# Block 0's second product split at 8 of 16 tiles of d_ff, and the transfers and casts around it put in another order

## The chip, the cores and the metric

The kernel runs on one core of a Trainium2 chip. The core has five engines that run side by side, each through its own instructions in order: TensorE (PE in the profile; PEld is its weight load), VectorE (DVE), ScalarE (ACT), GpSimd (POOL) and SyncE (SP), which here only issues DMA transfers. The metric is the device time of one execution in microseconds, the lower the better.

## The reference

Two parts follow each other. The first is a recurrent retention layer over 4 batches, 8 heads, 768 positions and a head dimension of 64; the second is a two-layer network over the 3072 resulting rows of 512, with d_ff = 2048:

```python
for t in range(S):
    state = gamma * state + k[t] (outer) v[t]        # per batch and head, 64 x 64
    y[t] = q[t] @ state / sqrt(D)
x = y.transpose(0, 2, 1, 3).reshape(3072, 512)
h = x @ w_in                                         # 512 -> 2048
g = maximum(h, 0) + alpha * minimum(h, 0)
out = g @ w_out                                      # 2048 -> 512
```

## The kernel before

All matmuls are in float16. The recurrence is computed in chunks: inside a chunk a masked product of q and k (the scores) is multiplied with v, and a state of 64 x 64 per head is carried from chunk to chunk. The 3072 rows are six blocks of 512 tokens. Blocks 0 and 1 are made of the units 0 to 3, each of 256 positions, two to a block; the later blocks are made of units of 128 positions that are numbered from 8.

For a unit of 256 positions the steps are: `uload` (three transfers of 512 KB for k, q and v), `uscaled` (k and q times powers of gamma, cast to float16 in tile `ukq`, four products on POOL for units 2 and 3), a turn of `ukq` into `ukT` (for unit 2 by transposing matmuls, `uturn`, whose banks are copied out by DVE and ACT; for unit 3 by two transposing transfers, `uturn_dma`), `ucast` (v to float16, ACT), `uscores` (PE, reads `ukT`), `umasked` (DVE, writes `um`), `ustates` and `usums` (the state), and `uoutputs` (PE, then copies into `xT`, which is the input of the network).

For a block of 512 tokens the first product `x @ w_in` runs over 16 tiles of d_ff (`ffn1`, `ffn1_half`; ACT makes `hm`, DVE makes the tile `gt`, `gs` for block 0). The second product of block 0 is cut in two: `ffn2_start` takes the first tiles of d_ff, summed in four banks of PSUM, one for each 128 rows, and ACT copies the four sums to `os`; `ffn2(0, lo=...)` takes the other tiles, and DVE adds the sums to `os`. Between the two parts stands the first half of block 1's first product. For blocks 1 to 5 the second product is `seven`, seven smaller products on sums of quarters of `g` (`g_sums`) and of w_out (`w_sums`: wsum0 from tiles 0 to 7, wsum1 and wsum2 in two halves each, wsum3).

The weights arrive as float32 in quarters of 1 MB, each as two transfers of 512 KB (`load_w`), and are cast to float16 by POOL (`cast_w`, four casts for a quarter). Quarter i of w_out holds the tiles 4i to 4i + 3 of d_ff. All of these loads, the transposing transfers and the stores are issued by SP in one order and go through one queue; the float32 data of loads and weights share a ring of 12 buffers of 512 KB.

The order of the work is written out by hand: each engine executes in the order of the lines of the kernel. The products are generators that yield after every matmul, and `tick(gen, m)` puts m of these matmuls between other work. Thus in `ffn2_start` the number of ticks ahead of `uturn`, `uscores`, `ustates` and `uoutputs` says how many of its matmuls PE does before each of them. An engine that stands at an instruction whose input is not there yet does nothing else meanwhile.

Of the kernel before, what the change touches and what calls it, by code (L numbers as in the profile page):

```python
# [19 lines left out]
def kernel(  # L20
# [310 lines left out]
    def uload(w, nms="kqv", parts=1):  # L331
        b, c = divmod(w, NCH // 2)
        for nm in nms:
            src = {"k": k, "q": q, "v": v}[nm]
            t = ring(f"{nm}u{w}").rearrange("p (h j d) -> p h j d", j=2, d=D)
            for r in range(2):
                ustaged[w, nm, r] = t[:, 4 * r : 4 * r + 4]
            n = H // parts
            for h in range(0, H, n):
                nc.sync.dma_start(  # L340
                    out=t[:, h : h + n],
                    in_=src[b, h : h + n, 256 * c : 256 * c + 256, :].rearrange(
                        "h (p j) d -> p h j d", j=2
                    ),
                )

    def uscaled(w, nm, r, eng):
        if w not in ukq:
            ukq[w] = sbp.tile([128, 2, 2, 4, 2, D], F16, tag="ukq", bufs=2, name=f"ukq{w}")
            ukT[w] = sbp.tile([128, 2, 4, 2, 128], F16, tag="ukT", bufs=2, name=f"ukT{w}")  # L350
            uv[w] = sbp.tile([128, 2, 4, 2, D], F16, tag="uv", bufs=2, name=f"uv{w}")
        a = "kq".index(nm)
        at = 32 + 16 * a + 8 * r
        eng.tensor_tensor(  # L354
            out=ukq[w][:, a, :, :, r, :].rearrange("p j i d -> p i j d"),
            in0=ustaged.pop((w, nm, r)),
            in1=tab[:, at : at + 8]
            .rearrange("p (i j) -> p i j", j=2)
            .unsqueeze(3)
            .to_broadcast([128, 4, 2, D]),  # L360
            op=MULT,
        )
# [34 lines left out]
    def uturn_dma(w):  # L397
        by_dma.add(w)
        for a in range(2):
            nc.sync.dma_start_transpose(  # L400
                out=ukT[w][:, a].rearrange("p i x n -> p (i x n)").rearrange(
                    "p (b n) -> p b n", n=128
                ),
                in_=ukq[w][:, a].rearrange("p j i r d -> p (j i r d)"),
            )
# [187 lines left out]
    def uoutputs(w):  # L593
        z = [None if w % (NCH // 2) == 0 else ps("za"), ps("zb")]
        uout_states(w, 1, z=z)
        zc = [b and z_copy(b).rearrange("p (a j n) -> p a j n", j=2, n=64) for b in z]
        uout_inner(w)
        uout_states(w, 0)
        uout_copy(w, z=zc)
# [128 lines left out]

    def ffn2_start(n):
        banks = [ps("ops", tag="pb") for _ in range(UB)]  # L730
        for f0 in range(0, 12, 4):
            for tq in range(UB):
                for ft in range(f0, f0 + 4):
                    nc.tensor.matmul(  # L734
                        out=banks[tq],
                        lhsT=gt_at(n, ft, slice(128 * tq, 128 * tq + 128)),
                        rhs=w_out_all[:, ft, :],
                        start=(ft == 0),
                        stop=(ft == 11),
                    )  # L740
                    if ft == 11:
                        os_sb = sbp.tile([128, d_model], FP, tag="os", bufs=5, name="os")
                        nc.scalar.activation(
                            out=os_sb, in_=banks[tq], func=COPY, bias=0.0, scale=1.0
                        )
                        partial[n, tq] = os_sb
                    yield
# [12 lines left out]
    def w_sums(which, eng, parts=None):  # L760
        i = which
        if i not in wsum:
            tag, bufs = (("ws0", 1), ("ukq", 2), ("ukT", 2), ("ukT", 2))[i]
            wsum[i] = sbp.tile([128, HF, 256], F16, tag=tag, bufs=bufs, name=f"wsum{i}")
        n = HF if parts is None else HF // 2
        for p in [0] if parts is None else parts:
            w_sum(i, eng, slice(n * p, n * p + n))
# [259 lines left out]
    def tick(gen, m):  # L1027
        for _ in range(m):
            if next(gen, 1) == 1:
                return  # L1030
# [21 lines left out]
    def load_w(nm, i, parts=2):  # L1052
        n = 4 // parts
        for j in (0, 2):
            t = ring(f"{nm}{i}{j}").rearrange("p (j d) -> p j d", j=2)
            if nm == "wi":
                src = wi[:, j : j + 2, 512 * i : 512 * i + 512]
            else:
                src = wo[:, 4 * i + j : 4 * i + j + 2, :]
            for jj in range(0, 2, n):  # L1060
                nc.sync.dma_start(out=t[:, jj : jj + n], in_=src[:, jj : jj + n])
            for jj in range(2):
                wst[nm, i, j + jj] = t[:, jj]

    def cast_w(nm, i, engs):
        left = [j for j in range(4) if (nm, i, j) in wst]
        for j, eng in zip(left, engs):
            to = w_in_all[:, j, 512 * i : 512 * i + 512] if nm == "wi" else w_out_all[:, 4 * i + j, :]
            t = wst.pop((nm, i, j))
            if eng is nc.scalar:  # L1070
                eng.activation(out=to, in_=t, func=COPY, bias=0.0, scale=1.0)
            else:
                eng.tensor_copy(out=to, in_=t)  # L1073
# [17 lines left out]
    V, G, A = nc.vector, nc.gpsimd, nc.scalar  # L1091
# [56 lines left out]
    busy(2, tag="pb")  # L1148
    uturn(1, "k", shared=True, first=A)
    ucast(0, 0, A)  # L1150
    load_w("wo", 1)
    busy(2, tag="pb")
    uturn(1, "q", shared=True)
    umasked(0, 1, sc[1], rs=(1,))
# [30 lines left out]
                pass  # L1185
    cast_w("wi", 2, [G, G, G, G])
    cast_w("wi", 3, [G, G, G, G])
    load_w("wo", 2)
    cast_w("wo", 0, [G, G, G, G])
    cast_w("wo", 1, [G, G, G, G])  # L1190
    uscaled(2, "k", 0, G)
    uscaled(2, "k", 1, G)
    uscaled(2, "q", 0, G)
    uscaled(2, "q", 1, G)
    uload(3)
    load_w("wo", 3)
    for _ in ffn1(0, lo=4):
        pass
    w_sums(0, V)
    gen = ffn2_start(0)  # L1200
    ucast(2, 0, A)
    ucast(2, 1, A)
    cast_w("wo", 2, [G, G, G, G])
    tick(gen, 24)
    uturn(2, "k", tag="pa", shared=True)
    tick(gen, 6)
    uturn(2, "q", tag="pa", shared=True)
# [1 line left out]
    sc = [uscores(2, 0), uscores(2, 1)]  # L1209
    umasked(2, 0, sc[0])  # L1210
    umasked(2, 1, sc[1])
    tick(gen, 4)
    ustates(2, tag="pa")
    usums(2)
    uscaled(3, "k", 0, G)
    uscaled(3, "k", 1, G)
    uscaled(3, "q", 0, G)
    uscaled(3, "q", 1, G)
    uturn_dma(3)
    for u in range(8, 11):  # L1220
        load(u)
    tick(gen, 5)
    uoutputs(2)
    ucast(3, 0, A)
    ucast(3, 1, A)
    w_sums(1, G, [0])
    cast_w("wo", 3, [G, G])
    w_sums(2, G, [0])
    cast_w("wo", 3, [G, G])
    for _ in gen:  # L1230
        pass
    gen = ffn1_half(1, 0)
# [8 lines left out]
    scaled(9, "q", G)  # L1241
    scaled(10, "k", G)
    scaled(10, "q", G)
    sc = [uscores(3, 0), uscores(3, 1)]
    umasked(3, 0, sc[0])
    tick(gen, 8)
    umasked(3, 1, sc[1])
    scaled(8, "k", A)
    cast(8, A)
# [1 line left out]
    turn(9)  # L1251
    load(11)
    turn(10)
    adds = []
    last = ffn2(0, lo=12, late=adds)
    tick(last, 13)
    uoutputs(3)
    flush(adds)
    cast(9, A)
    for _ in last:  # L1260
        pass
# [185 lines left out]
```

## Time and profile before

| | us |
|---|---|
| median of 3 runs (lowest, highest) | 197.95 (197.07, 199.46) |
| the profiled execution's own time | 198.98 |
| its span, first to last instruction | 197.0 |
| PE busy in the span | 189.3 |
| POOL busy | 147.5 |
| DVE busy | 151.3 |
| ACT busy | 121.7 |

The span of the profiled execution is 2.0 us shorter than its time. PE is the engine that is busy for most of the span, so that time is lost only where PE waits; the tensor clock was granted in full throughout. The other engines have idle time, but what they deliver late makes PE wait. Queue q1, on which SP issues, moved 37.36 of the 38.78 MB.

### The profile page before, as it was taken

The page shows a single profiled execution, that of the slowest core. Times are in us where ns is not written, and L with a number is a line of the kernel's source. Part 1 is how long each engine was busy: PE and PEld are TensorE (multiplying, and loading weights), DVE is VectorE, ACT ScalarE, POOL GpSimd, SP SyncE. Part 2 cuts the span into 40 slices and gives each one's busy share as a digit, 9 for nine tenths or more (in the row PEclk, how much of TensorE's full clock was granted, in tenths as well). Part 3 has the DMA queues.
Part 4 walks back from the last instruction along what each step waited for, and adds up shares of the span by engine and source line. Part 5 has one row for each costly group of instructions (what it writes and reads, how often), then busy time and mean ns, then how long its engine had stood idle before and what let it go on. Part 6 is the DMA issues. An engine that isn't in the chain of part 4 may idle for free.

```text
span 197.0 us, 6461 instructions
## 1 busy us (share of the span) xinstructions
PE 189.3 (96%) x2668; PEld 131.7 (67%) x2668; DVE 151.3 (77%) x260; ACT 121.7 (62%) x272; POOL 147.5 (75%) x148
## 2 busy tenths in 40 slices
PE   7789899999999989999999999999999999999993
PEld 5657444557768878744688754788754888654882
DVE  2597889253999698588897879968879977799943
ACT  3368664349687863476458988749987433687120
POOL 3286788999996955999659999579999397589000
PEclk9999999999999999999999999999999999999999
DMA  6999999999999989899999999993890011200014
GB/s 168 310 336 350 404 396 296 332 358 179 210 230 148 214 257 272 196 215 299 196 231 228 226 185 265 237 221 93 113 263 2 3 57 63 100 3 0 2 57 160
DMA packets 92749, 38.78 MB, mean 197 GB/s; under 512 B 70176, under 2 KB 88624, under 8 KB 92720
## 3 DMA queue, kind: packets, MB, share of 16 engines
q1 hardware_dynamic: 91440, 37.36, 77.2%
q10 hardware_dynamic: 1280, 1.01, 1.5%
q8 instruction: 21, 0.34, 0.7%
q14 instruction: 8, 0.07, 0.1%
HBM read 27.35 MB, written 6.29 MB: 171 GB/s over the span
## 4 chain that ended last, share of the span: by engine, by line
PE 73%; SPq 10%; DMA 7%; POOL 6%; DVE 1%; issue 1%; POOLq 0%
PE ops L809 30%; PE hps L942 16%; PE hps L632 12%; PE hps L972 5%; SPq L340 4%; SPq L117 4%; DMA wi<-in_moe_w_in_dram 4%; PE ops L734 4%; POOL wsum L757 3%; DMA kqs<-in_q_dram 3%; PE ya L293 1%; PE yb L293 1%; POOL gs L757 1%; DVE gs L757 1%; POOL ukq L354 1%; PE sca L234 1%
## 5 line engine op out<-in xcount | busy, mean ns | idle before, releaser
L809 PEld LDWEIGHTS <-gt 128*128 128x128 f16 x320 | 30.6, 98 | 4.2
L942 PE MATMUL hps<-xT,win 128*128 128x512 f16 x144 | 33.0, 379 | 0.0
L929 DVE SCALAR_TENSOR_TENSOR gt<-hm,small,hps 128x512 f16<-128x512 f32 (+1 forms) x42 | 28.7, 706 | 5.1 <-ACT hm L925 3.8
L809 PE MATMUL ops<-wout,gt 128*128 128x256 f16 x240 | 28.4, 273 | 0.0
L925 ACT ACTIVATE hm<-hps 128x512 f32<-128x512 f32 x39 | 23.1, 593 | 6.1 <-PE hps L942 5.4
L632 PE MATMUL hps<-xT,win 128*128 128x512 f16 x112 | 24.7, 379 | 0.6 <-POOL win L1073 0.6
L137 POOL TENSOR_TENSOR kq<-kqs,tab 128x512 f16<-128x512 f32 x23 | 23.7, 1051 | 1.9 <-DMA kqs<-in_q_dram 1.9
L642 DVE SCALAR_TENSOR_TENSOR gt<-hm,small,hps 128x512 f16<-128x512 f32 x28 | 20.9, 748 | 3.8 <-ACT hm L641 0.9
L942 PEld LDWEIGHTS <-win 128*128 128x128 f16 x144 | 14.1, 98 | 14.5
L641 ACT ACTIVATE hm<-hps 128x512 f32<-128x512 f32 x28 | 16.7, 597 | 8.9 <-PE hps L632 8.6
L674 DVE SCALAR_TENSOR_TENSOR gt<-hm,small,hps 128x256 f16<-128x256 f32 x40 | 16.9, 476 | 5.0 <-ACT hm L669 5.0
L827 ACT ACTIVATE kept<-ops 128x512 f32<-128x512 f32 x15 | 9.0, 597 | 18.8 <-PE ops L809 18.7
L632 PEld LDWEIGHTS <-win 128*128 128x128 f16 x112 | 10.9, 98 | 13.6 <-POOL win L1073 1.1
L809 PE MATMUL ops<-wsum,gs 128*128 128x256 f16 x160 | 19.0, 273 | 0.7 <-DVE gs L757 0.7
L217 POOL TENSOR_TENSOR t<-ss,tab 128x256 f16<-128x256 f32 x13 | 8.7, 669 | 13.6 <-DVE ss L215 13.6
L757 POOL TENSOR_TENSOR gt<-gt,gs 128x1024 f16<-128x1024 f16 x8 | 17.0, 2126 | 2.2 <-DVE gs L757 2.2
L660 PE MATMUL hps<-xT,win 128*128 128x256 f16 x160 | 18.4, 273 | 0.0
L129 ACT ACTIVATE kq<-kqs,tab 128x64 f16<-128x64 f32 x72 | 18.0, 336 | 0.0
L660 PEld LDWEIGHTS <-win 128*128 128x128 f16 x160 | 15.4, 98 | 2.6 <-DVE xT L584 0.3
L809 PEld LDWEIGHTS <-gs 128*128 128x128 f16 x160 | 15.1, 98 | 3.0 <-DVE gs L757 1.0
L669 ACT ACTIVATE hm<-hps 128x512 f32<-128x512 f32 x20 | 11.8, 597 | 4.5 <-PE hps L660 4.4
L839 DVE TENSOR_TENSOR os<-ops,kept 128x512 f32<-128x512 f32 (+1 forms) x17 | 10.5, 624 | 5.0 <-ACT kept L827 3.7
(139 smaller groups left out, 391.5 us busy)
## 6 DMA issues: line engine op xcount, KB each, us to landing
out_dram<-os SPq DMA_DIRECT2D x20, 256.0 KB, 3.6
wi<-in_moe_w_in_dram SPq DMA_DIRECT2D x8, 512.0 KB, 8.6
wo<-in_moe_w_out_dram SPq DMA_DIRECT2D x8, 512.0 KB, 8.7
kqs<-in_k_dram SPq DMA_DIRECT2D x16, 256.0 KB, 4.4
kqs<-in_q_dram SPq DMA_DIRECT2D x16, 256.0 KB, 4.3
vs<-in_v_dram SPq DMA_DIRECT2D x16, 256.0 KB, 4.7
ku<-in_k_dram SPq DMA_DIRECT2D x4, 256.0 KB, 4.4
qu<-in_q_dram SPq DMA_DIRECT2D x4, 256.0 KB, 5.3
```

Source lines behind the costliest of these rows:

```text
L129: eng.activation(out=kqs[u][:, a, h % 4, h // 4, :], in_=staged[u][nm][:, h, :], func=COPY, bias=0.0, scale=tab[:, H * a + h : H * a + h + 1],
L137: eng.tensor_tensor(out=kqs[u][:, a].rearrange("p i r d -> p r i d"), in0=staged[u][nm].rearrange("p (r i) d -> p r i d", i=4), in1=tab[:, ...
L632: nc.tensor.matmul(out=hps, lhsT=w_in_all[:, hp, 128 * ft : 128 * ft + 128], rhs=xT[n][:, :, hp, :], start=(hp == 0), stop=(hp == 3),)
L641: nc.scalar.activation(out=hm, in_=hps, func=RELU, bias=0.0, scale=-1.0)
L642: nc.vector.scalar_tensor_tensor(out=gt_at(n, ft, slice(0, TB)), in0=hm, scalar=oma_sb[:, ft : ft + 1], in1=hps, op0=MULT, op1=ADD,)
L660: nc.tensor.matmul(out=hps[:, 256 * (ft - f0) : 256 * (ft - f0) + 256], lhsT=w_in_all[:, hp, 128 * ft : 128 * ft + 128], rhs=xT[n][:, half ...
L674: nc.vector.scalar_tensor_tensor(out=gt_at(n, f, to), in0=hm[:, at], scalar=oma_sb[:, f : f + 1], in1=hps[:, at], op0=MULT, op1=ADD,)
L757: eng.tensor_tensor(out=out, in0=a, in1=b, op=op)
L809: nc.tensor.matmul(out=bk[:, 256 * t : 256 * t + 256], lhsT=a[:, f, 128 * t : 128 * t + 128], rhs=w[:, f, :], start=first and f == 0 and ( ...
L925: nc.scalar.activation(out=t, in_=src, func=RELU, bias=0.0, scale=-1.0)
L929: nc.vector.scalar_tensor_tensor(out=gt_at(n, f, cols), in0=hm, scalar=oma_sb[:, f : f + 1], in1=src, op0=MULT, op1=ADD,)
L942: nc.tensor.matmul(out=hps, lhsT=w_in_all[:, hp, 128 * ft : 128 * ft + 128], rhs=x[:, :, hp, :], start=(hp == 0), stop=(hp == 3),)
```

## The change

Block 0's second product is cut after 8 instead of 12 of the 16 tiles: `ffn2_start` has 32 matmuls instead of 48, and `ffn2(0, lo=8)` has 32 instead of 16. The number of matmuls, copies and adds is the same. With `ffn2_start` shorter, unit 2's steps stand after fewer of its matmuls: 3 ahead of `uturn` for k (24 before), then 6, 4, 5 (4 before) and 6 (5 before). Unit 3's scores stand after 54 instead of 48 matmuls of the first half of block 1's first product, and its outputs after 18 of the 32 matmuls of `ffn2(0, lo=8)` (13 of 16 before). The delayed add of `tq == 2` goes.

On the side of the transfers, w_out's second quarter is loaded after unit 2 instead of ahead of it, unit 3 is loaded right behind that quarter, and unit 3's two transposing transfers stand between the third and the fourth quarter instead of behind the fourth. POOL's casts and products follow that order. The sum wsum0, on DVE, moves from ahead of `ffn2_start` to behind unit 2's outputs.

```diff
     def ffn2_start(n):
         banks = [ps("ops", tag="pb") for _ in range(UB)]
-        for f0 in range(0, 12, 4):
+        for f0 in range(0, 8, 4):
...
-                        stop=(ft == 11),
+                        stop=(ft == 7),
                     )
-                    if ft == 11:
+                    if ft == 7:
...
     ucast(0, 0, A)
-    load_w("wo", 1)
     busy(2, tag="pb")
...
     cast_w("wi", 3, [G, G, G, G])
-    load_w("wo", 2)
+    load_w("wo", 1)
+    uload(3)
     cast_w("wo", 0, [G, G, G, G])
-    cast_w("wo", 1, [G, G, G, G])
     uscaled(2, "k", 0, G)
     uscaled(2, "k", 1, G)
     uscaled(2, "q", 0, G)
     uscaled(2, "q", 1, G)
-    uload(3)
-    load_w("wo", 3)
+    cast_w("wo", 1, [G, G, G, G])
+    load_w("wo", 2)
     for _ in ffn1(0, lo=4):
         pass
-    w_sums(0, V)
     gen = ffn2_start(0)
     ucast(2, 0, A)
     ucast(2, 1, A)
-    cast_w("wo", 2, [G, G, G, G])
-    tick(gen, 24)
+    uscaled(3, "k", 0, G)
+    uscaled(3, "k", 1, G)
+    uscaled(3, "q", 0, G)
+    uscaled(3, "q", 1, G)
+    uturn_dma(3)
+    load_w("wo", 3)
+    tick(gen, 3)
     uturn(2, "k", tag="pa", shared=True)
     tick(gen, 6)
     uturn(2, "q", tag="pa", shared=True)
...
     umasked(2, 1, sc[1])
-    tick(gen, 4)
+    tick(gen, 5)
     ustates(2, tag="pa")
     usums(2)
-    uscaled(3, "k", 0, G)
-    uscaled(3, "k", 1, G)
-    uscaled(3, "q", 0, G)
-    uscaled(3, "q", 1, G)
-    uturn_dma(3)
+    cast_w("wo", 2, [G, G, G, G])
     for u in range(8, 11):
         load(u)
-    tick(gen, 5)
+    tick(gen, 6)
     uoutputs(2)
+    w_sums(0, V)
     ucast(3, 0, A)
     ucast(3, 1, A)
     w_sums(1, G, [0])
-    cast_w("wo", 3, [G, G])
     w_sums(2, G, [0])
-    cast_w("wo", 3, [G, G])
+    cast_w("wo", 3, [G, G, G, G])
     for _ in gen:
         pass
...
+    tick(gen, 6)
     sc = [uscores(3, 0), uscores(3, 1)]
     umasked(3, 0, sc[0])
-    tick(gen, 8)
+    tick(gen, 2)
     umasked(3, 1, sc[1])
...
-    adds = []
-    last = ffn2(0, lo=12, late=adds)
-    tick(last, 13)
+    last = ffn2(0, lo=8)
+    tick(last, 18)
     uoutputs(3)
-    flush(adds)
     cast(9, A)
```

The order in which SP issues transfers, from w_out's second quarter to the first loads of unit 8, was this; `wo10` and `wo12` are the two halves of quarter 1 of w_out, `ku2` is k of unit 2, `ukT3` the turned k and q of unit 3, `kqs8` k and q of unit 8:

```order
L1061 DMA wo10_267<-in_moe_w_out_dram 128x2x512
L1061 DMA wo12_269<-in_moe_w_out_dram 128x2x512
L340 DMA ku2_464<-in_k_dram 128x8x128
L340 DMA qu2_466<-in_q_dram 128x8x128
L340 DMA vu2_468<-in_v_dram 128x8x128
L1061 DMA wo20_592<-in_moe_w_out_dram 128x2x512
L1061 DMA wo22_594<-in_moe_w_out_dram 128x2x512
L340 DMA ku3_611<-in_k_dram 128x8x128
...
L1061 DMA wo30_617<-in_moe_w_out_dram 128x2x512
L1061 DMA wo32_619<-in_moe_w_out_dram 128x2x512
L400 DMA_TRANSPOSE ukT3_872<-ukq3_871 128x8x128 x2
L117 DMA kqs8_880<-in_k_dram 128x8x64
```

SP's order at the same place is now this:

```order
L340 DMA qu2_462<-in_q_dram 128x8x128
L340 DMA vu2_464<-in_v_dram 128x8x128
L1061 DMA wo10_588<-in_moe_w_out_dram 128x2x512
L1061 DMA wo12_590<-in_moe_w_out_dram 128x2x512
L340 DMA ku3_592<-in_k_dram 128x8x128
...
L1061 DMA wo20_613<-in_moe_w_out_dram 128x2x512
L1061 DMA wo22_615<-in_moe_w_out_dram 128x2x512
L400 DMA_TRANSPOSE ukT3_716<-ukq3_715 128x8x128 x2
L1061 DMA wo30_724<-in_moe_w_out_dram 128x2x512
L1061 DMA wo32_726<-in_moe_w_out_dram 128x2x512
L117 DMA kqs8_856<-in_k_dram 128x8x64
```

Each of the units 2 and 3 has one quarter of w_out fewer ahead of it, and the two transposing transfers have passed the fourth quarter; whatever stands behind `wo32` has the same transfers ahead of it as before.

On POOL, from unit 3's products (`ukq3`) to the first product of unit 8 (`kq8`), the order was this:

```order
L354 TENSOR_TENSOR ukq3_871<-ku3_611,tab_63 128x4x2x64 x2
L354 TENSOR_TENSOR ukq3_871<-qu3_613,tab_63 128x4x2x64 x2
L757 TENSOR_TENSOR wsum1_964<-wout_68,wsum0_717 128x1024
L1073 CAST wout_68<-wo30_617 128x512 x2
L757 TENSOR_TENSOR wsum2_968<-wout_68 128x1024
L1073 CAST wout_68<-wo32_619 128x512 x2
L757 TENSOR_TENSOR wsum1_964<-wout_68,wsum0_717 128x1024
L137 TENSOR_TENSOR kq8_1043<-kqs8_880,tab_63 128x2x4x64
```

From the casts of w_out's third quarter (`wo20`, `wo22`) to the same product it is now:

```order
L1073 CAST wout_68<-wo20_613 128x512 x2
L1073 CAST wout_68<-wo22_615 128x512 x2
L757 TENSOR_TENSOR wsum1_945<-wout_68,wsum0_941 128x1024
L757 TENSOR_TENSOR wsum2_947<-wout_68 128x1024
L1073 CAST wout_68<-wo30_724 128x512 x2
L1073 CAST wout_68<-wo32_726 128x512 x2
L757 TENSOR_TENSOR wsum1_945<-wout_68,wsum0_941 128x1024
L137 TENSOR_TENSOR kq8_1027<-kqs8_856,tab_63 128x2x4x64
```

Unit 3's products have moved ahead of the third quarter's casts, and both half sums (wsum1, wsum2) now stand ahead of all four casts of the fourth quarter.

## The prediction

> **What bounds the kernel now.** I read the page's busy times first:
>
> ```profile
> PE 189.3 (96%) x2668; PEld 131.7 (67%) x2668; DVE 151.3 (77%) x260; ACT 121.7 (62%) x272; POOL 147.5 (75%) x148
> ```
>
> PE does nearly nothing but its own work, and the change leaves its matmuls as they are (48 + 16 becomes 32 + 32). So it can only take away or add waits of PE. Which there are, the list of PE's waits says (engine, line, whom it waited for: us in total, times, longest):
>
> ```profile
> PE ops L809 <- DVE gs L757: 0.7, 1, 0.7
> PE hps L632 <- POOL win L1073: 0.6, 1, 0.6
> ```
>
> The second waits for a transfer of w_in that stands ahead of all that is moved. The first is what there is to be had at this place. What ends last there, the chain of waits shows (start, us, what):
>
> ```profile
> 55.55 5.82 DMA kqs<-in_q_dram
> 61.37 0.07 issue
> 61.44 1.04 POOL kq L137
> 62.49 4.17 POOL wsum L757 x2
> 66.65 2.09 POOL gs L757
> 68.77 1.30 DVE gs L757 x2
> 70.09 0.70 DVE gs L757
> 70.80 0.05 issue
> 70.84 3.23 PE ops L809 x28
> ```
>
> A late transfer of unit 10's q, then POOL, then DVE let PE go on at 70.84. Next PE's timeline around the change (start, us, what, idle before):
>
> ```profile
> 31.69 5.34 PE L734 MATMUL ops<-wout,gt 128*128 128x512 f16 x24
> 36.87 0.61 PE L383 MATMUL trb<-mi,ukq 128*128 128x128 f16 x8
> 37.32 1.46 PE L734 MATMUL ops<-wout,gt 128*128 128x512 f16 x6
> ...
> 47.67 3.67 PE L660 MATMUL hps<-xT,win 128*128 128x256 f16 x32
> 51.27 0.24 PE L483 MATMUL sca<-ukT 64*64 64x128 f16 x2
> ...
> 52.73 2.97 PE L696 MATMUL ops<-wout,gt 128*128 128x512 f16 x13
> ...
> 56.16 0.22 PE L526 MATMUL yb<-um,uv 64*64 64x128 f16 x2
> 56.45 0.24 PE L526 MATMUL ya<-um,uv 64*64 64x128 f16 x2
> ...
> 70.84 3.23 PE L809 MATMUL ops<-wsum,gs 128*128 128x256 f16 x28 [0.68 <-DVE gs L757]
> ```
>
> From 31.69 on PE goes without a gap, but for 0.68 ahead of 70.84 (it could have gone on at 70.16) and some 0.2 ahead of 56.45 (these outputs of unit 3 otherwise follow each other by 0.05). So at most about 0.9 us can be gained. From these rows also the prices of a step of PE: (36.87 - 31.69)/24 = 0.216 us for a matmul of 512 columns, (51.27 - 47.67)/32 = 0.11 for one of 256, 0.45 for eight transposes.
>
> **The change part by part.**
>
> *The queue.* The rate of the DMA queue, by windows (start:end, length, busy time of PE, PEld, DVE, ACT, POOL, clock, DMA share, GB/s), before, within and after the pair of transposing transfers:
>
> ```profile
> 22.00:28.00 6.00, 6.00 (x29) 2.72 (x28) 5.27 (x8) 4.17 (x8) 5.27 (x10) 1.00 1.05 404
> 43.00:44.00 1.00, 1.00 (x47) 0.64 (x48) 0.28 (x1) 0.71 (x3) 1.00 (x2) 1.00 1.05 387
> ...
> 46.00:47.00 1.00, 1.00 (x12) 0.89 (x10) 0.00 (x0) 1.00 (x4) 1.00 (x3) 1.00 0.19 40
> ...
> 48.00:49.00 1.00, 1.00 (x12) 0.89 (x11) 0.90 (x3) 1.00 (x4) 1.00 (x1) 1.00 1.76 93
> ```
>
> The queue is full, so a quarter of w_out (2 x 512 KB) that is no longer ahead saves what stands behind it 1.05 MB / 404 GB/s = 2.6 us. And the transposing pair holds the queue: in 46 to 47 and 48 to 49 it moves almost nothing, and I take the hold to end at 49.1. Their landing, and that of unit 3's v just ahead, from the tile's view (SP's issues, first and last start; then issue to landing) and from the issue of v:
>
> ```profile
> L400 SPq DMA_TRANSPOSE ukT<-ukq x2: 1337/1940/2542, 42.3 to 44.3; - x2
> ...
> DMA to landing us min/median/max: 5.7/5.9/6.2
> ```
>
> ```profile
> 35.20 3.33 SPq L340 DMA_DIRECT2D vu<-in_v_dram  x1
> ```
>
> ```profile
> vu<-in_v_dram SPq DMA_DIRECT2D x1, 512.0 KB, 7.9
> ```
>
> The second transposing transfer landed at 44.3 + 6.2 = 50.5, unit 3's v at 35.2 + 7.9 = 43.1. With 2.6 taken off: v at 40.5, the halves of the third quarter, at 387 GB/s 1.35 apart, at 41.85 and 43.2, the turned unit 3 at 47.9, the hold's end at 46.5, and the fourth quarter behind it at 47.85 and 49.2.
>
> *POOL and DVE.* Their timelines:
>
> ```profile
> 27.62 4.93 POOL L1073 CAST wout<-wo 128x512 f16<-128x512 f32 x8 [0.50 <-DMA wo<-in_moe_w_out_dram]
> 32.95 3.02 POOL L354 TENSOR_TENSOR ukq<-ku,tab 128x512 f16<-128x512 f32 x2 [0.40 <-DMA ku<-in_k_dram]
> ...
> 40.23 2.04 POOL L354 TENSOR_TENSOR ukq<-ku,tab 128x512 f16<-128x512 f32 x2
> ...
> 49.50 1.17 POOL L1073 CAST wout<-wo 128x512 f16<-128x512 f32 x2
> ...
> 61.44 1.04 POOL L137 TENSOR_TENSOR kq<-kqs,tab 128x512 f16<-128x512 f32 x1 [1.54 <-DMA kqs<-in_q_dram]
> ```
>
> ```profile
> 33.18 1.89 DVE L757 TENSOR_TENSOR wsum<-wout 128x2048 f16<-128x2048 f16 x1
> ...
> 44.69 0.44 DVE L584 TENSOR_TENSOR xT<-yb,zs 128x256 f16<-128x256 f32 x1
> ```
>
> **Unit 2's turn.** k of unit 2 let POOL start at 32.95; 2.6 earlier is 30.35, behind the first quarter's casts, which end at 27.62 + 4.93/2 = 30.1. Two products cost 2.04 (row at 40.23): k is ready at 32.4, q at 34.4. PE arrives at the turn of k after 3 instead of 24 matmuls, at 31.69 + 3 x 0.216 = 32.35, and waits 0.1; at that of q after 0.45 + 6 x 0.216 more, at 34.2, and waits 0.25. Together **+0.35**. If the queue serves unit 2 half a microsecond sooner it is 0, half a microsecond later 0.85. The 21 matmuls that hid POOL here before are gone, so each delay of k and q counts in full. The second quarter, behind unit 2, is cast by 37.5 by the same steps; PE asks for its first tile at 37.1 and for its last at 38, across `ustates`: I cost this at nothing, POOL's casts being 0.6 apart and the first done at 35.3.
>
> **Unit 3's scores.** PE is there 16 x 0.216 = 3.46 sooner and 6 x 0.11 later: 51.27 - 3.46 + 0.66 + 0.35 = 48.8. The transposing pair lands at 47.9: no wait, with 0.9 to spare. POOL has unit 3's products done 2.6 earlier, at 40.23 + 4 x 1.02 - 2.6 = 41.7, before the queue comes to the pair at 43.2.
>
> **wsum0 beside the casts.** The two products at 32.95 took 3.02 instead of 2.04, and what ran beside them is wsum0 on DVE: it stopped POOL for 1.0. It now starts when unit 2's outputs are copied, at 45.1 less 19 matmuls (4.1) plus 0.35, so at 41.4, and ends at 43.3. That is where POOL casts the third quarter (41.85, 43.2). I let the casts begin at 43.3: four of 0.585 end at 45.6.
>
> **The fourth quarter.** Then come two half sums of 2.08 each (half of the row at 62.49): 49.8. Its data is there at 49.2. The casts are done at 50.4, 51.0, 51.55 and 52.1. PE begins `ffn2(0, lo=8)` 0.8 after the scores (52.73 - 51.27 less the six matmuls that now stand ahead), at 49.6, and wants the first of these tiles four matmuls later, at 50.45, the last at 51.1. It waits until 52.1: **+1.0**. This is the largest term and the least certain. Without the stop by wsum0 POOL is 1.0 earlier and the term is 0; with the fourth quarter's data only behind the landed pair (47.9 + 2.7 = 50.6) the last cast ends at 51.9, about as late as now.
>
> **Unit 3's outputs** come 18 matmuls and that wait behind 49.6, at 54.5, 5.7 after the scores. The mask that they waited for was there 5.2 after the scores (56.45 - 51.27), and DVE has the same work ahead of it: the 0.2 goes, **-0.2**.
>
> **POOL's chain to 70.84.** The fourth quarter's casts ended at 49.50 + 1.17 = 50.7 and now at 52.1, 1.4 later. POOL waited 1.54 for unit 10's q ahead of 61.44, which swallows this. As the transfers ahead of the loads of units 8 to 10 are the same in number, q lands where it did: DVE again lets PE go at about 70.84.
>
> **Sum.** PE arrives at 70.16 + 0.35 + 1.0 - 0.2 = 71.3 where it left at 70.84: **+0.5**. The old wait there disappears, eaten by new ones. Behind 71 each step is ordered as before and PE has no gap, so the end moves by the same. The profiled execution would take 198.98 + 0.5 = 199.5; it lies 1.0 above the median of the three runs, so against the median I say 197.95 + 0.4 = 198.3. With the terms at their ends (0 to 0.85, 0 to 1.2) PE arrives between 69.96 and 72.0, but never goes on before the gate at about 70.84 unless q lands sooner: -0.2 to +1.2.
>
> **Rivals.**
>
> *The hidden gain comes.* If the transposing pair costs the queue no more than its bytes, 2 x 256 KB, 1.3 us at 404 GB/s, all behind it lands sooner: the fourth quarter at 43.2 + 1.3 + 2.7 = 47.2, and unit 10's q some 3 us before 61.37 (the pair now takes 50.5 - 43.1 - 2.7 = 4.7). Then POOL's casts wait for the half sums alone, and the gate opens 0.7 or more sooner; with unit 2 served in time PE goes on at 69.96: -0.9, 197.1. For it: 1.54 of idle POOL at 61.44 hang on one transfer. Against it: the 40 and 93 GB/s. The Trainium skill ("Advanced Engine Details and Errata", X-Bar Transpose) says that transposing DMAs are as fast as regular ones on trn2. By that rule this rival would be the forecast; the two slices speak against it here. Chance 0.2.
>
> *The pair lands no sooner.* If the two transposing transfers are held by something other than the fourth quarter (SP stands at them until POOL and the queue let them go, with the fourth quarter's loads now behind them on SP), they land at 50.5 as before and the fourth quarter 1.35 and 2.7 behind, at 53.2. PE waits 1.7 at unit 3's scores, and POOL's last cast ends at 54.4 where PE wants it at 51.1 + 1.7 = 52.8: 1.6 more. Sum 70.16 + 0.35 + 1.7 + 1.6 - 0.2 = 73.6, +2.8: 200.7. It decides the sign beyond 1% from a last half landing at about 52.4. For it: the second issue took 2.54 instead of 1.34 in the row above, so something held SP. Against it: POOL is done with unit 3 at 41.7. Chance 0.14. In this case the change would also not do what it says, since the pair would be between the quarters only in the program.
>
> **Numbers.** The forecast's case (197.7 to 199.2) has 0.62, the gain 0.2, the pair 0.14, and 0.04 I leave to what I don't see. A measurement of this kernel, whose three runs lie between 197.07 and 199.46, can't tell less than about 1% from no change. Faster by over 1% would need 195.97: the bound of 0.9 excludes it but for the spread, 0.03. Slower by over 1% (199.93) is most of the pair's case and a little of the spread: 0.13. The range leaves out most of the pair's case and reaches down to the gain: 197.0 to 200.2.
>
> **What would show it.** In the changed profile: (1) the wait at L809 for DVE's gs is gone or under 0.3; (2) PE waits at L383 for POOL's ukq, 0 to 0.85 in sum; (3) PE's L696 waits for POOL's casts of w_out, about 1; (4) no wait of L483 for the transposing transfers, which land near 48; (5) POOL's casts of the third quarter are stretched beside wsum0. I am wrong if L483 waits, if the pair's landing hasn't moved, or if PE's busy time itself changes.

## The result and the profile after

The changed kernel took 199.69 us (median of 22 runs, 198.23 to 200.95) beside 198.6 us for the kernel before (22 runs on the same chip, 197.07 to 202.39). The ratio is 1.0065 with a 95% interval of 1.0042 to 1.0089: slower by 1.3 us, between 0.8 and 1.8. The ratio leaves out the executions that took over 1.5% longer than the fastest of their kernel. The time is within the 1% named as no change and within the range, but 1.4 above the predicted 198.3 and 0.5 above the upper end of the likeliest case (199.2). The profiled execution took 200.02, its span 198.1.

First the busy times of the profile after:

```profile
PE 189.0 (95%) x2668; PEld 131.6 (66%) x2668; DVE 152.5 (77%) x260; ACT 121.7 (61%) x272; POOL 146.6 (74%) x148
```

PE's work is the same (189.3 before); only its waits moved. Its list of waits, same columns as before:

```profile
PE trb L383 <- DVE ukq L354: 2.5, 2, 1.7
...
PE sca L483 <- DMA ukT<-ukq: 0.7, 1, 0.7
PE ops L696 <- POOL wout L1073: 0.6, 3, 0.3
```

The wait for gs at L809 is gone. The first row is units 0 and 1 in the front, which the change doesn't touch. The other two are new, and both stand at the changed place: unit 3's scores wait for the transposing pair, and the second product waits for the fourth quarter's casts. PE's timeline there:

```profile
49.96 0.24 PE L483 MATMUL sca<-ukT 64*64 64x128 f16 x2 [0.71 <-DMA ukT<-ukq]
...
50.76 1.34 PE L696 MATMUL ops<-wout,gt 128*128 128x512 f16 x5
52.28 0.38 PE L696 MATMUL ops<-wout,gt 128*128 128x512 f16 x1 [0.18 <-POOL wout L1073]
52.93 0.38 PE L696 MATMUL ops<-wout,gt 128*128 128x512 f16 x1 [0.27 <-POOL wout L1073]
53.49 2.53 PE L696 MATMUL ops<-wout,gt 128*128 128x512 f16 x11 [0.18 <-POOL wout L1073]
...
71.78 1.47 PE L809 MATMUL ops<-wsum,gs 128*128 128x256 f16 x12
```

Seven matmuls lie between 50.76 and 53.49; at 0.216 they would take 1.5, they took 2.7: 1.2 lost, more than the waits named in the rows. The matmuls with gs begin at 71.78 (69.56 before) without a wait; the fifth of them, for which PE waited until 70.84 before, comes at 72.2. What POOL does in that time:

```profile
40.66 2.04 POOL L354 TENSOR_TENSOR ukq<-qu,tab 128x512 f16<-128x512 f32 x2
44.30 1.17 POOL L1073 CAST wout<-wo 128x512 f16<-128x512 f32 x2 [1.61 <-DMA wo<-in_moe_w_out_dram]
45.66 1.17 POOL L1073 CAST wout<-wo 128x512 f16<-128x512 f32 x2 [0.19 <-DMA wo<-in_moe_w_out_dram]
46.91 2.12 POOL L757 TENSOR_TENSOR wsum<-wout,wsum 128x1024 f16<-128x1024 f16 x1
49.00 2.12 POOL L757 TENSOR_TENSOR wsum<-wout 128x1024 f16<-128x1024 f16 x1
51.06 2.38 POOL L1073 CAST wout<-wo 128x512 f16<-128x512 f32 x4
...
63.26 4.20 POOL L757 TENSOR_TENSOR wsum<-wsum,wout 128x1024 f16<-128x1024 f16 x2
67.63 2.13 POOL L757 TENSOR_TENSOR gs<-gt 128x1024 f16<-128x1024 f16 x1 [0.17 <-DVE gt L674]
```

POOL stands for 1.61 until the third quarter lands, and then has no gap until gs. And the pair's tile (first and last issue, then issue to landing):

```profile
L400 SPq DMA_TRANSPOSE ukT<-ukq x2: 1397/2110/2824, 40.7 to 42.7; - x2
...
DMA to landing us min/median/max: 6.8/6.9/7.1
```

The second transfer landed at 42.7 + 7.1 = 49.8, where 47.9 was predicted and the kernel before had 50.5: the pair hardly came sooner. What SP does meanwhile (start, us, what):

```profile
33.36 3.59 SPq L340 DMA_DIRECT2D vu<-in_v_dram  x1
...
40.73 4.82 SPq L400 DMA_TRANSPOSE ukT<-ukq  x2
45.60 1.12 SPq L1061 DMA_DIRECT2D wo<-in_moe_w_out_dram  x2
```

SP begins the second transposing issue at 42.7, when POOL has made its data (40.66 + 2.04), stands in it for 2.8, and only then, at 45.60, issues the fourth quarter.

### The profile page after: what moved, and what is told of

It is laid out like the page before. It is cut to its first block, busy times and chain, and to the rows that moved or that the text cites. A ratio compares the mean times of both kernels' runs of the same rounds, so it can differ in the third digit from the quotient of the medians.

```text
span 198.1 us, 6460 instructions
## 1 busy us (share of the span) xinstructions
PE 189.0 (95%) x2668; PEld 131.6 (66%) x2668; DVE 152.5 (77%) x260; ACT 121.7 (61%) x272; POOL 146.6 (74%) x148
## 4 chain that ended last, share of the span: by engine, by line
PE 87%; POOL 5%; DMA 3%; DVE 2%; SPq 1%; issue 0%; POOLq 0%
PE ops L809 32%; PE hps L942 16%; PE hps L632 11%; PE hps L660 8%; PE hps L972 5%; DMA qu<-in_q_dram 3%; PE ops L696 3%; PE ops L734 3%; POOL wsum L757 2%; POOL ukq L354 2%; PE trb L383 1%; PE ya L293 1%; POOL wout L1073 1%; PE sca L234 1%; PE yb L293 1%; PE wps L1045 1%
## 5 line engine op out<-in xcount | busy, mean ns | idle before, releaser
L809 PEld LDWEIGHTS <-gt 128*128 128x128 f16 x320 | 30.6, 98 | 4.1
L809 PE MATMUL ops<-wout,gt 128*128 128x256 f16 x240 | 28.4, 273 | 0.0
L827 ACT ACTIVATE kept<-ops 128x512 f32<-128x512 f32 x15 | 9.0, 597 | 17.9 <-PE ops L809 17.8
L809 PE MATMUL ops<-wsum,gs 128*128 128x256 f16 x160 | 18.8, 273 | 0.0
L809 PEld LDWEIGHTS <-gs 128*128 128x128 f16 x160 | 15.2, 98 | 2.1
```

The lines of the kernel that those rows point to most:

```text
L809: nc.tensor.matmul(out=bk[:, 256 * t : 256 * t + 256], lhsT=a[:, f, 128 * t : 128 * t + 128], rhs=w[:, f, :], start=first and f == 0 and ( ...
```

## Experiments

Two accounts stood against each other. Theory A: what costs is that stream of loads around the transposing pair, by PE's waits and by POOL's chain behind the third quarter. Rival C: the cost lies elsewhere, in the split itself, or in the front, where PE of the changed kernel was 1.7 us later at its first matmul with w_in (18.71 against 17.05).

**The same kernels again.** No edit.

> The changed kernel once more, nothing edited. In its first profile PE begins w_out's first product at 32.58 us where the kernel before begins at 31.69, though the change touches no instruction ahead of it; it then waits 0.88 for unit 3's transposing pair and 1.1 for POOL's casts of the fourth quarter. Theory A (the 0.9 of the front is chance of that one execution, the cost is in the two waits): the product begins within 0.4 of 31.7, the two waits are there again at 0.6 to 1.2 each, and the ratio to the kernel before is 1.003 to 1.010. Rival B (the change delays the front, by the loads that are issued in another order): the product begins at 32.3 to 32.8 again.

> The kernel before, once more, for its profile. So far the first matmul with w_in begins at 17.05 us in it and at 16.65 to 18.71 in five profiles of the changed kernel and its variants, whose instructions up to there are the same. Theory A (the time of the front, and of the stream of loads, is chance of an execution): it begins between 16.6 and 18.7, unit 3's v lands within 1.2 of 43.1, and PE's only waits from 30 to 72 us are again those for DVE's um and gs, at most 1.3 together. Rival B (the change delays the front): it begins at 17.05 within 0.2.

> The changed kernel a third time, on the same chip as the three runs beside it, for a third profile of its place. In two profiles the waits of PE for the transposing pair were 0.88 and 0.92 (beyond the step's usual time) and for the fourth quarter's casts 1.1 and 2.1. Theory A (they belong to the change): both again, 0.6 to 1.2 and 0.6 to 2.2, and a ratio to the kernel before of 1.003 to 1.010. Rival (chance of two executions): one of them missing, and a ratio below 1.003.

The changed kernel's ratio was 1.0028 (0.9981 to 1.0074, 12 runs) and 1.0065 (1.0025 to 1.0104, 12 runs). The first matmul with w_in began at 17.86 and 16.69 in these two profiles and at 17.14 in the kernel before's second one, and between 16.6 and 17.8 in all variants below: the late front was chance of that execution (after waits of 0.8 and 1.7 in the front its clock stood at 0.5 from 10.8 to 14.2), and w_out's first product began at 31.73 and 31.14, as A said and not B. The first ratio lies just below the range that A named, and the casts cost 2.1 in that profile, above A's 1.2; of the two accounts ahead of the third profile neither came whole. Of the two waits one stayed in all three profiles and one didn't. PE's rows in the third:

```profile
47.81 0.24 PE L483 MATMUL sca<-ukT 64*64 64x128 f16 x2
...
48.61 1.55 PE L696 MATMUL ops<-wout,gt 128*128 128x512 f16 x5
50.33 0.38 PE L696 MATMUL ops<-wout,gt 128*128 128x512 f16 x1 [0.18 <-POOL wout L1073]
50.98 0.38 PE L696 MATMUL ops<-wout,gt 128*128 128x512 f16 x1 [0.28 <-POOL wout L1073]
51.54 2.53 PE L696 MATMUL ops<-wout,gt 128*128 128x512 f16 x11 [0.18 <-POOL wout L1073]
```

The scores don't wait here; the casts cost 51.54 - 48.61 - 1.5 = 1.4 (2.1 in the second profile). The reason is in the pair's tile, in this third profile:

```profile
L400 SPq DMA_TRANSPOSE ukT<-ukq x2: 1330/1868/2405, 39.2 to 41.2; - x2
...
DMA to landing us min/median/max: 5.2/5.8/6.4
```

It landed at 41.2 + 5.2 = 46.4, 3.4 sooner than in the first profile and 1.4 before PE came. So the wait at L483 (0.7, 0.8, 0) is a matter of the execution, that at L696 (1.2, 2.1, 1.4) is not. The kernel before, a second time, had in PE's list of waits for DVE's masks

```profile
PE ya L526 <- DVE um L513: 0.4, 2, 0.2
```

and both of these stand in the front (at 15.64 and 16.18). From 30 to 72 us its list is empty: the 0.7 for gs on which the prediction set its base was absent in this execution (197.13 us).

What the changed place costs can be read from two stretches of PE's timeline: from the first matmul of `ffn2_start` to the fifth with gs (31.69 to 70.84 in the first profile of the kernel before), and from there to the end of the span.

| us | first stretch | the rest |
|---|---|---|
| kernel before, two profiles | 39.15, 38.30 | 126.1, 125.9 |
| changed kernel, three profiles | 39.64, 41.13, 39.13 | 125.9, 126.7, 125.9 |

On the average the first stretch is 1.2 longer and the rest 0.1; without the second profile of the changed kernel, an execution of 201.52, the first is 0.7 longer and the rest no longer. So the loss sits in the changed place and not in the front.

**The order of loads without the split.**

```
-        for f0 in range(0, 8, 4):          (and stop, copy at tile 7)
+        for f0 in range(0, 12, 4):         (at tile 11)
-    last = ffn2(0, lo=8);  tick(last, 18)
+    last = ffn2(0, lo=12, late=adds);  tick(last, 13)  ...  flush(adds)
```

> The split undone: ffn2_start takes 12 tiles again and ffn2 the last 4 (13 matmuls ahead of unit 3's outputs, one addition late, as before the change), the loads and casts in the changed kernel's order. Theory A (only PE's waits on casts and landings count): PE comes to the third quarter's tiles at 42.7 but POOL has them cast at 44.9 to 46.8, so PE waits about 3.5 at L734, and then for nothing at L483 and L696, where it is 3.5 us later: 3.5 - 2.0 = 1.5 slower than the changed kernel, 201.2. Rival C (the split itself costs the 1.3, by the order of products and copies): about 1 faster than the changed kernel, 198.6.

202.31 us, ratio 1.0164 (1.0101 to 1.0227): 3.2 slower than before, so C falls for the split, and A's direction holds. PE's rows at the third quarter:

```profile
39.76 1.67 PE L734 MATMUL ops<-wout,gt 128*128 128x512 f16 x7
44.12 0.38 PE L734 MATMUL ops<-wout,gt 128*128 128x512 f16 x1 [2.68 <-POOL wout L1073]
...
45.40 3.85 PE L734 MATMUL ops<-wout,gt 128*128 128x512 f16 x10 [0.34 <-POOL wout L1073]
```

Nothing waits at L483 or L696, as expected. The last row holds an unexpected term: 10 matmuls in 3.85 us instead of 2.2. The windows (columns as in the prediction) say why; the granted clock, third from the end, is 0.52:

```profile
46.00:48.50 2.50, 2.50 (x7) 0.85 (x7) 0.00 (x0) 0.82 (x2) 2.50 (x2) 0.52 1.08 356
```

**The split without the order of loads.** The same lines changed the other way in the kernel before.

```
-        for f0 in range(0, 12, 4):
+        for f0 in range(0, 8, 4):
-    adds = [];  last = ffn2(0, lo=12, late=adds);  tick(last, 13);  uoutputs(3);  flush(adds)
+    last = ffn2(0, lo=8);  tick(last, 18);  uoutputs(3)
```

> Of the change only the split: the kernel before with ffn2_start over 8 tiles and ffn2 over the other 8 (18 matmuls ahead of unit 3's outputs, no late addition); loads, casts and the transposing pair in the order of before. Theory A (the moved loads are needed once the split is at 8): PE is 3.5 us earlier at unit 3's scores, about 47.7, the pair lands where it did, 49.1 to 50.5, so PE waits 1.4 to 2.7 at L483, besides up to 0.5 at unit 2's masks, whose cover is gone; the fourth quarter, cast by 50.7, holds nobody: about 2 slower than before, 200.5. Rival C (the split is free, the changed order of loads is what costs): within 0.4 of before.

201.37 us, ratio 1.0135 (1.0073 to 1.0196): the size was right, the place wrong. Unit 3's scores lost 0.3. PE waited in unit 2's chain instead, whose masks, states and copies had lost the matmuls that stood among them:

```profile
PE hps L660 <- ACT xT L585: 1.1, 1, 1.1
PE zb L526 <- DVE ut L444: 0.7, 1, 0.7
...
PE sta L423 <- DVE um L494: 0.5, 1, 0.5
PE stb L423 <- DVE um L494: 0.4, 1, 0.4
```

The profiled execution was one of the longest of its six (202.94, mean clock 0.982: it stood at 0.5 from 43.5 to 50.3; one at full clock took 199.53), so I take the places from it and not the size. Each half of the change alone was slower than both together (for the split alone the intervals overlap).

**The pair behind the fourth quarter.**

```
-    uturn_dma(3)
     load_w("wo", 3)
+    uturn_dma(3)
```

> The transposing pair behind the fourth quarter instead of ahead of it, all else as in the changed kernel. Theory A (the pair holds the queue for some 4.7 us wherever it stands, and delays what is queued around it): third quarter at about 43 and 44.3 instead of 44.25 and 45.61, fourth at 45.6 to 47.2 instead of 50.9 and 52.2, pair near 50.5; PE waits about 1.4 at L483 and 0 to 0.3 at L696, 2.0 in the changed kernel together: 0.6 faster than the changed kernel, about 199.1. Rival B (the pair costs only its bytes): pair landed near 48.5, neither wait, 2 faster, 197.7. Rival C (the cost lies elsewhere, with the order of PE's work): no difference to the changed kernel.

202.13 us, ratio 1.0177 (1.0118 to 1.0236): 2.4 slower than the changed kernel where 0.6 faster was expected. The landings were near what A said (third quarter 41.9 and 43.3, fourth 45.6 and 47.0, first transfer of the pair 49.5; the landing of the second is not in the trace, and PE went on at 51.0), so B falls. But PE came to the scores at 47.0 and not at 49.1, the front of this execution being 2.1 shorter, and so waited much longer; and then the clock dropped again. PE's row, and two windows:

```profile
51.01 0.24 PE L483 MATMUL sca<-ukT 64*64 64x128 f16 x2 [3.92 <-DMA ukT<-ukq]
```

```profile
47.00:51.00 4.00, 0.08 (x1) 0.02 (x1) 1.01 (x3) 0.11 (x1) 4.00 (x5) 1.00 1.29 185
...
52.50:56.00 3.50, 3.50 (x10) 1.31 (x9) 2.95 (x6) 2.58 (x10) 3.50 (x3) 0.54 1.01 229
```

**The pair on ACT's queue.**

```
-            nc.sync.dma_start_transpose(        (called ahead of load_w("wo", 3))
+            nc.scalar.dma_start_transpose(      (called behind uoutputs(2))
```

> The changed kernel with the transposing pair issued by ACT, on ACT's queue, after unit 2's outputs are copied (about 43 us), instead of by SP among w_out's quarters. Theory A1 (the pair holds the queue that it stands in): third and fourth quarters land as without a pair, 2 to 6.3 us after unit 3's v, the pair near 47, no wait at L483, at most 0.5 at L696: 1.5 faster than the changed kernel, 198.2. Theory A2 (the pair holds the 16 DMA engines, whichever queue it stands in): the fourth quarter lands 9 to 11 us after unit 3's v as in the changed kernel, and the time stays within 0.5 of 199.7.

204.11 us, ratio 1.0286 (1.0239 to 1.0334). The quarters landed as without a pair (41.6 to 46.5), as A1 said; the pair did not land near 47 but at 50.8, and the time was lost at a place that neither theory had: ACT itself. Its timeline, and PE's list of waits:

```profile
40.50 5.54 ACTq L400 DMA_TRANSPOSE ukT<-ukq  x2
46.09 1.15 ACT L367 ACTIVATE uv<-vu 128x512 f16<-128x512 f32 x2 [5.19 <-issue]
```

```profile
PE sta L423 <- ACT uv L367: 4.0, 2, 3.7
```

```profile
38.98 2.04 POOL L354 TENSOR_TENSOR ukq<-qu,tab 128x512 f16<-128x512 f32 x2
```

The data of the pair was done on POOL at 38.98 + 2.04 = 41.0, and the issue of the two transfers still held ACT until 46.0; the cast of unit 3's v behind it held PE. So the hold sits also at the issuing engine. For SP, which has only loads behind it, the same shows as loads that are issued late: in the changed kernel the second issue took 2.8 (the tile's row above) from 42.7 on, when its data was done too. Plain loads are held in their issue as well: 3.6 for unit 3's v in the row above, 2.9 and 3.6 for two loads that SP issued in this run beside ACT's pair. In the first and the third profile of the changed kernel the issue of unit 3's v ended within 0.1 of the landing of the second quarter, and the second transposing issue within 0.1 of the landing of the third; in the second profile the latter ended 0.4 ahead of it. What holds an issue was not tested. Whether the 16 DMA engines are held besides can't be told from this run.

**No pair: unit 3 turned by PE.** Two forms; the second has the transposes earlier and their copies on ACT alone.

```
-    uturn_dma(3)
-    tick(gen, 32)
+    tick(gen, 24);  uturn(3, "k", tag="pa", shared=True)
+    tick(gen, 8);   uturn(3, "q", tag="pa", shared=True)
```

```
-    uturn_dma(3)
-    tick(gen, 32)
+    tick(gen, 8);   uturn(3, "k", tag="pa", shared=True, first=A)
+    tick(gen, 8);   uturn(3, "q", tag="pa", shared=True, first=A);  tick(gen, 16)
```

> No transposing pair at all: unit 3 is turned by PE (16 transposes in two groups among ffn1_half, after 24 and 32 of its matmuls), all else as in the changed kernel. PE has 0.9 us of work more (0.45 for eight). Theory A (the pair's hold of the queue is what costs): third quarter landed by 43 and 44.3, fourth by 47, no wait of PE at L483 and L696: 0.9 - 2.0 = 1.1 faster than the changed kernel, 198.6, the wait for DVE's gs back at L809 with 0 to 0.7. Rival C (the cost lies elsewhere): 0.9 slower than the changed kernel, 200.6.

> No transposing pair, unit 3 turned by PE, as in pe_turn, but the two groups of transposes stand after 24 and 32 of ffn1_half's 64 matmuls by a count that ends 16 matmuls before the scores, and ACT alone copies their results, since PE waited 1.0 for DVE's copy in pe_turn. PE has 0.9 us of work more than in the changed kernel. Theory A (the pair's hold of the queue costs what was read, 2.0): waits of at most 0.3 at L483 and 0.6 at L696: 0.8 faster than the changed kernel, about 198.9. Rival C (the pair is not what costs): no faster than pe_turn, 200.3 or more.

200.33 us, ratio 1.0093 (1.0060 to 1.0126), and 199.66 us, 1.0066 (1.0030 to 1.0102). In the first form PE waited 1.0 for DVE's copy of the turned q, a wait of my own making. In the second, this row of PE's list is all that is left of the waits at L483 and L696, and POOL no longer stands ahead of the third quarter, the more so as its products of q were stretched from 2.04 to 3.03 beside wsum0:

```profile
PE ops L696 <- POOL wout L1073: 0.2, 1, 0.2
```

```profile
38.70 3.03 POOL L354 TENSOR_TENSOR ukq<-qu,tab 128x512 f16<-128x512 f32 x2
41.69 2.28 POOL L1073 CAST wout<-wo 128x512 f16<-128x512 f32 x4
...
48.20 2.29 POOL L1073 CAST wout<-wo 128x512 f16<-128x512 f32 x4
```

Without the pair the fourth quarter's second half lands 2.5 and 2.7 us behind the third's; with the pair between them 5.2 to 6.9 in the seven profiles that have it there. So with the pair between them the two quarters land 2.6 to 4.3 us further apart. How much of this is the pair's own movement is not shown. Without it SP issues the fourth quarter right behind the third, at 37.1 in the second form, and with it at 45.60 in the first profile of the changed kernel, after it has stood at the pair; in the prediction's row for 46 to 47 (kernel before), where the pair was taken to hold the queue, the DMA engines were busy for 0.19 of the time. And of the ten profiles in which both landings are known, the second transposing transfer landed 0.8 to 0.9 behind the first in five, no more than loads of 256 KB take there (0.9), and 2.3 to 2.5 in the others. But the fourth quarter's casts begin 6.5 after the third's here too, with the data there since 45.1: they stand behind POOL's two half sums (4.2), not behind the transfer. The time of the second form is the changed kernel's (199.53 on the same chip), half way between what A and C said, that of the first is near C's 200.6; so the times don't bear A out. The waits do, and the two stretches in part: the second form's took 38.69, with PE's 0.9 of transposes in it, where the changed kernel took 39.1 to 41.1; but its rest took 126.85 where that kernel's took 125.9 to 126.7, with a wait of PE of 0.5 for nothing that the profile shows. These are figures of one execution.

**Other work in the waits, and POOL relieved.** First PE's waits are covered (unit 3's scores 8 matmuls later; tiles 8 to 11 of all four token quarters ahead of tiles 12 to 15):

```
-    tick(gen, 6);  sc = [uscores(3, 0), uscores(3, 1)]
+    tick(gen, 14); sc = [uscores(3, 0), uscores(3, 1)]
-    last = ffn2(0, lo=8)
+    last = ffn2_end(0, 8)    # for f0 in (8, 12): for tq in range(4): for ft in range(f0, f0 + 4)
```

then ACT takes two casts from POOL:

```
-    cast_w("wo", 3, [G, G, G, G])
+    cast_w("wo", 3, [G, G])
     ...
     umasked(3, 1, sc[1])
+    cast_w("wo", 3, [A, A])     # and the second half sums and scaled(8..10) behind it
```

then unit 2's turn comes later:

```
-    tick(gen, 3);  uturn(2, "k", tag="pa", shared=True)
+    tick(gen, 9);  uturn(2, "k", tag="pa", shared=True)
```

> The changed kernel with other work put into PE's two new waits: unit 3's scores come after 62 instead of 54 of ffn1_half's 64 matmuls (8 matmuls, 0.9 us, before them), and ffn2's rest takes tiles 8 to 11 of all four token quarters before tiles 12 to 15 (the fourth quarter is wanted 12 matmuls, 2.6 us, later). Loads, POOL and DVE as in the changed kernel. Theory A (the late fourth quarter reaches PE on two ways: by the waits and by POOL's chain of casts, half sums and gs): no wait at L483, at most 0.3 at L696, but PE now waits 0.8 to 1.8 for DVE's gs at L809, so it is only 0.2 to 0.9 faster than the changed kernel, 199.1. Rival B (the two waits are the whole cost): 2.0 faster, 197.7.

> The kernel covered, and ACT casts two of the four tiles of the fourth quarter (0.6 us each, behind unit 3's masks), so that POOL has 1.2 us less ahead of its half sums and gs. Theory A (POOL's chain is what then bounds this place): gs comes 0.6 to 1.2 sooner than in covered and the wait at L809 shrinks by it, 198.3. Rival B (POOL's chain doesn't bound): no difference to covered.

> The kernel relief, and unit 2's turn of k after 9 instead of 3 matmuls of ffn2_start (1.3 us later), which puts back some of the cover that PE had over POOL's products of unit 2. Theory A (all that the change adds is waits that other work can cover): no wait of L383 for POOL's ukq of unit 2 (0.96 in relief, 0.25 to 0.9 in the changed kernel), none at L483 and L696, at most 0.5 at L809: 0.3 to 0.9 faster than relief, 198.2, level with the kernel before. Rival C (something else of the change costs 1 us): no faster than relief, 198.8.

198.83 us (1.0028, 0.9992 to 1.0065), 198.76 (1.0038, 1.0008 to 1.0069) and 199.24 (1.0033, 0.9992 to 1.0073). The covered kernel still waits 0.4 at L483 (none was expected), not at all at L696, and the wait for gs is back. Its rows of PE at gs (L832 here, L809 before), and POOL's last step ahead of it:

```profile
68.87 0.61 PE L832 MATMUL ops<-wsum,gs 128*128 128x256 f16 x4 [0.47 <-DVE gs L780]
70.20 2.03 PE L832 MATMUL ops<-wsum,gs 128*128 128x256 f16 x17 [0.72 <-DVE gs L780]
```

```profile
65.95 2.13 POOL L780 TENSOR_TENSOR gs<-gt 128x1024 f16<-128x1024 f16 x1
```

That is A's expectation (0.8 to 1.8 there; 199.1). POOL no longer waits for anybody ahead of gs: it is itself late. One more wait, at 106.9, is in this profile and at that step in none of the changed kernel's three; the profile shows nothing that it was for ("issue"):

```profile
PE ops L832 <- issue: 1.2, 1, 1.2
```

With 1.2 of casts taken from it only one of the two waits is left:

```profile
69.83 2.36 PE L832 MATMUL ops<-wsum,gs 128*128 128x256 f16 x20 [0.43 <-DVE gs L780]
```

The wait shrank as A said, but the time did not follow (0.1, well inside the intervals; the wait without a shown cause is 0.5 here), nor with unit 2's turn later: there PE waited 0.6 for ACT's copy of unit 2's outputs, 0.4 for the second quarter's casts and 0.6 for gs. None of these beats the kernel before, and the three lie close enough to the changed kernel (1.0042 to 1.0089) that the gain of some 0.6 us is likely and not shown. Not tried was the one order that the POOL rows point to for the cast term, the fourth quarter's casts ahead of the half sums.

## Why the prediction was right or wrong

**PE's work unchanged, only its waits move:** right, 189.0 against 189.3.

**Unit 2's turn, +0.35:** right. PE's rows there:

```profile
33.67 1.46 PE L734 MATMUL ops<-wout,gt 128*128 128x512 f16 x6
35.19 0.62 PE L383 MATMUL trb<-mi,ukq 128*128 128x128 f16 x8
```

From one to the other are 1.52 us, for six matmuls that take 1.30: 0.2 lost for POOL's products; 0.6 and 0.25 in the other two profiles.

**Unit 3's scores, no wait:** the step that failed, by "the turned unit 3 at 47.9"; by the prediction's own sign ("I am wrong if L483 waits") it failed in two profiles of three. They have 49.8, 49.6 and 46.4, and waits of 0.7, 0.8 and none; the kernel before had 50.5 and, in its second profile, 49.1. Two steps ahead of it were too short. "2.6 taken off" all that stands behind the removed quarter: unit 3's v landed at 41.5, 42.0 and 40.0 instead of 40.5. And the third quarter's second half, costed at 2.7 behind v, lands 3.6 to 4.6 behind it with the pair next in the queue and 3.0 to 3.6 without. The first profile of the kernel before had this already, in the quarter that stood between v and the pair there:

```profile
L1061 SPq DMA_DIRECT2D wo<-in_moe_w_out_dram x2: 511/930/1350, 38.6 to 40.1; - x2
...
DMA to landing us min/median/max: 7.0/7.1/7.1
```

Its second half landed at 40.1 + 7.1 = 47.2, 4.0 behind v (43.1) and not 2.7; so the pair stood 3.3 behind that quarter and not 4.7. POOL's products of unit 3, expected by 41.7, were done at 42.7, 44.2 and 41.2. A lead of 0.9 was no cover against landings that vary by 3 us between executions of one kernel.

**wsum0 stretching the third quarter's casts:** did not happen. The casts came later (44.30) than wsum0 ended (43.8), and took 1.17 a pair. In the second profile wsum0 fell on POOL's products of unit 3's q instead: they took 3.02, not 2.04, and the second transposing issue began at 44.2.

**The fourth quarter, +1.0:** measured 1.2, 2.1 and 1.4. The way was the one drawn, casts behind two half sums on POOL, but what moved the half sums was the third quarter's landing (45.6 for its second half instead of 43.2) and not wsum0. "Data is there at 49.2" was off by 3 (52.2) and cost nearly nothing beside POOL; the run without a pair shows the casts as late with the data long there. Of my two ways for the end of the pair's hold, the discarded one is borne out: the fourth quarter lands 2.4 to 4.1 behind the pair's landing.

**Unit 3's outputs, -0.2:** right; the gap of 0.2 is in both profiles of the kernel before and in none of the three.

**POOL's chain: "this swallows it":** failed. The 1.54 that POOL waited for unit 10's q were to absorb its delay. But now POOL begins later: it stands until the third quarter lands (1.6, 0.4 and 1.3 in the three profiles) and then is busy with hardly a gap. So DVE had gs ready 39.2, 40.7 and 38.7 after the first matmul of `ffn2_start`, where the kernel before had it ready after 39.1 and 37.9: on the average 1.1 later. The 1.54 itself was of one execution: in the second profile of the kernel before POOL did not wait there. PE, delayed on its own way by POOL's casts, came to gs no sooner, and so the list of waits shows nothing there. The covered kernel took PE's delay away and found the other one.

**The sum, +0.5, measured +1.3:** besides the scores and the larger cast term, the base was one execution. The 0.7 that was to be eaten by the new waits is there in one profile of the kernel before and not in the other, so on the average there was less to eat. And of the 1.4 between the forecast 198.3 and the measured 199.69, 0.65 is the base: the median of the kernel before was 197.95 in three runs and 198.6 in 22. So it is shown where the time is lost and by which waits; why the loads around the pair land as late as they do, by the pair's own movement or because SP stands at its issue, stays open.

**The rivals.** The hidden gain did not come: with the pair between them two quarters land 2.6 to 4.3 us further apart, where its bytes at 404 GB/s would be 1.3. The Trainium skill's rule ("Advanced Engine Details and Errata", X-Bar Transpose) that transposing DMAs are as fast as regular ones fits five of the ten profiles here, where the second transfer of 256 KB within SBUF landed 0.8 to 0.9 behind the first, and not the five with 2.3 to 2.5. The case in which the pair lands no sooner (3.3 of new waits at scores and casts, +2.8) came half true in two of the three profiles: the pair was late, at 49.8 and 49.6, and the two waits came to 1.9 and 2.9. Its mechanism is seen in SP's rows: SP stands at the second transfer until 45.5, with the fourth quarter's loads behind it. It was worth more than the chance of 0.14.

## What to carry to other kernels

Before taking matmuls away from between a transfer and its user, count the cover against the spread of the landing (here some 3 us between executions), not against one trace. Where two engines run the same stretch without a gap, price a late transfer on both: PE's waits showed one side of it, POOL's chain had the other, and covering the first only brought out the second. Ask also what stands behind a transfer on the engine that issues it. And a wait in a profile of one execution is no sure thing to be won.

## What the runs showed of the hardware

A long wait of PE cost more than itself. After 3.9 us of waiting (pair behind the fourth quarter) the granted clock stood at 0.54, and after 2.7 us (split undone) at 0.52, in the windows shown above; after 3.7 us (pair on ACT's queue) it was

```profile
48.00:52.00 4.00, 4.00 (x20) 2.85 (x19) 2.77 (x7) 2.51 (x6) 3.92 (x6) 0.51 1.25 256
```

At half speed 3.5 us do the work of 1.75, and the times fit that price, though the longer waits are in them too: of the six executions with the pair behind the fourth quarter the one with a mean clock of 1.0 took 200.6, those at 0.99 took 202.0 to 203.4 and the one at 0.981 took 205.3; with the split undone it was 200.0 at 1.0 and 201.1 to 202.8 at 0.991 to 0.992. The single waits of 0.7 to 1.0 at this place in the other profiles are followed by no drop. The Trainium skill ("TensorE: Matmul & The Clock Gate", HAM oscillation) warns of idle gaps over about 3.4 us between matmuls; here 2.7 with shorter waits behind it were enough. With the split alone the clock stood at 0.5 from 43.5 to 50.3, after four waits of 0.2 to 0.7 between 40 and 43, so one long wait is not needed; what the least is, these runs don't show.

The other surprise is that the issue of a transfer can hold the engine that issues it: ACT stood at two transposing transfers until 5.0 us after their data was there, SP at one for 2.8, and SP at the plain load of unit 3's v for 3.6. On ACT, which has other work behind it, that stopped PE.
